# A conditional fallback and its branch hints: a constant hint on five engines against a register hint on two

## The chip, the cores and the metric

One core of one Trainium2 chip. The metric is the time of one execution in device microseconds; the profile's span of the same execution is 1.7 to 1.9 us shorter.

## The reference

Two attention blocks over the same input, mixed by a gate (batch 1, sequence 2048, width 512, 32 heads of 16):

```python
g = sigmoid((x * gate_w).sum(-1, keepdims=True))
a = full_softmax_attention(x, A_wqkv, A_wo)
b = sliding_attention(x, B_wqkv, B_wo)      # window 8, dilation 2
return g * a + (1 - g) * b
```

## The kernel before

A fast path of some 21,000 instructions computes everything, and also a flag that says whether its approximations were safe. Behind it stands an exact version of the whole computation, which runs only if the flag is set. With these inputs it is not set, so each engine loads the flag, jumps over a long body and ends. A branch hint is an instruction ahead of that branch, 49 to 56 ns long in the traces, that names the branch and a direction. A branch that has none is called a miss below: from its start to the engine's next instruction it takes longer than the 0.47 to 0.60 us with a hint.

```python
    with ExitStack() as c1:
        _Fast(c1, tc, aps, flag).build()
    cond = nc.values_load(flag[0:1, 0:1], min_val=0, max_val=1)
    with tc.If(cond > 0, label="exact"):
        tc.strict_bb_all_engine_barrier()
        with ExitStack() as c2:
            _build_exact(c2, tc, aps)
```

The head of the fast path loads x from two engines' queues, warms PE up with zeros and makes a zeroed tile for that:

```python
        nc.sync.dma_start(out=self.x_tiles[0][:, 0:2, :], in_=self.x_src[:, 0:2, :])
        nc.scalar.dma_start(out=self.x_tiles[0][:, 2:4, :], in_=self.x_src[:, 2:4, :])
        self.load_w("A", "q", 0)
        # ... cut: five more loads on SyncE, the gate vector last
        self.wz = c([P, P], BF16, name="wz")
        nc.vector.memset(self.wz[:, 0:P], 0.0)
        warm = self.wk.tile([P, 1], F32, name="warm")
        nc.vector.memset(warm[:], 0.0)
        nc.scalar.activation(out=warm[:], in_=warm[:], func=ACT.Exp)
```

In the body ScalarE runs 687 softmax activations, 628 of them behind a wait instruction of their own in this trace. The hint is placed from the loop that emits the instruction streams, at half of the work:

```python
            if p >= 1024 and not hinted:
                hinted = True
                tc.mark_branch_hint_location("exact", hint="LikelyTaken",
                                             engines=[ENG.SP, ENG.Activation, ENG.DVE, ENG.PE, ENG.Pool])
```

Of the kernel before, what the change touches and what calls it, by code (L numbers as in the profile page):

```python
# [11 lines left out]
ENG = mybir.EngineType  # L12
# [4 lines left out]
I32 = mybir.dt.int32  # L17
# [81 lines left out]
def _build_exact(ctx, tc, aps):  # L99
# [232 lines left out]
    if True:  # L332
# [76 lines left out]
        def b_softmax_ops():  # L409
# [46 lines left out]
            def fin():  # L456
# [4 lines left out]
                B["er_d"] = tc.dram_tile([P, WIN * 512 + 1024], BF16, name="er_dram")  # L461
                nc.sync.dma_start(out=B["er_d"][:], in_=er[:])
            return ([(setup, 0.8)] + [(mxw(w), 0.45) for w in range(2, WIN)] + [(sub(w), 0.4) for w in range(WIN)]
                    + [(exp_, 0.1)] + [(sumw(w), 0.7) for w in range(1, WIN)] + [(rcp(k), 0.5) for k in range(8)]
                    + [(fin, 1.2)])
# [289 lines left out]
class _Fast:  # L755
# [15 lines left out]
    def setup(self):  # L771
        nc, tc, ctx = self.nc, self.tc, self.ctx
# [68 lines left out]
        warm = self.wk.tile([P, 1], F32, name="warm")  # L841
        nc.vector.memset(warm[:], 0.0)
        nc.scalar.activation(out=warm[:], in_=warm[:], func=ACT.Exp)

        pidx = c([P, 1], I32, name="pidx")
        pi2 = c([P, 1], I32, name="pi2")
# [641 lines left out]
    def run(self):  # L1488
        nc, tc = self.nc, self.tc
# [8 lines left out]
        p = 0  # L1498
# [385 lines left out]
            return t["PE"] + 0.25  # L1884

        guard = 0
        hinted = False
        while True:
            guard += 1
            assert guard < 2000000  # L1890
# [13 lines left out]
                    moved = True  # L1904
            if p >= N and not self.steps and not aq and not any(pvq) and cur == NB:
                break
            if p >= 1024 and not hinted:
                hinted = True
                tc.mark_branch_hint_location("exact", hint="LikelyTaken",
                                             engines=[ENG.SP, ENG.Activation, ENG.DVE, ENG.PE, ENG.Pool])  # L1910
            eng = min(t, key=lambda e: t[e])
            now = t[eng]
            others = min(v for e, v in t.items() if e != eng)
# [205 lines left out]
```

## Time and profile before

| | before |
|---|---|
| time, median of 3 (later 4) runs | 703.44 us (703.24) |
| span in the profile | 701.2 us |
| first softmax activation | 9.28 us |
| ScalarE's last output issue | 696.64 us |
| busy: PE, ScalarE, VectorE | 97, 97, 94% |

Three stretches matter: the head up to the first softmax activation, the body from there to ScalarE's last output issue, and the tail from that issue to the end. Sequencer work (hints, branches, waits, loads of registers) is not counted as busy; it shows in the views by source line. There an engine's name with a q behind it is its sequencer.

### The profile page before, as it was taken

To read this page: it belongs to the slowest core of one execution; us is meant where nothing else is said; L and a number is where in the kernel's file an instruction comes from. 1 tells how busy PE (TensorE), PEld (TensorE's weight loads), DVE (VectorE), ACT (ScalarE), POOL (GpSimd) and SP (SyncE) were. 2 spreads that over 40 slices of the span, in tenths; PEclk is the share of its full clock that TensorE was granted. 3 is DMA by queue.
4 is the path that set the end of the run, shared out by engine and by line. 5 is a ranking of instruction groups with operands and counts; after the bars stand their busy time and mean duration, and the time that the engine had idled before them with its cause. 6 is when DMAs were issued, how large, how long until landed. Compare 5 with 4: busy or idle time off the path is not lost.

```text
span 701.2 us, 21355 instructions
## 1 busy us (share of the span) xinstructions
PE 681.1 (97%) x8578; PEld 218.6 (31%) x8578; DVE 658.5 (94%) x1099; ACT 677.9 (97%) x701; POOL 422.0 (60%) x358
## 2 busy tenths in 40 slices
PE   8999999999999999999999999999999999999996
PEld 4432222233332333233322232322222332222443
DVE  5999999998789999999999999999999999999975
ACT  5999999999999999999999999999999999999993
POOL 3556667677477545645557486676745765656680
PEclk9999999999999999999999999999999999999999
DMA  6001100000100100000003436355554553556641
GB/s 174 5 12 39 39 9 21 14 2 8 36 2 13 28 1 4 7 3 8 4 8 82 127 84 169 91 154 144 132 141 110 151 138 90 146 138 146 144 112 42
DMA packets 64486, 48.67 MB, mean 69 GB/s; under 512 B 22528, under 2 KB 64000, under 8 KB 64256
## 3 DMA queue, kind: packets, MB, share of 16 engines
q1 hardware_dynamic: 63680, 45.83, 25.5%
q8 instruction: 68, 1.11, 0.6%
q0 software_dynamic: 288, 1.05, 0.5%
q10 hardware_dynamic: 416, 0.39, 0.2%
q14 instruction: 34, 0.28, 0.2%
HBM read 39.85 MB, written 5.26 MB: 64 GB/s over the span
## 4 chain that ended last, share of the span: by engine, by line
PE 54%; ACT 30%; issue 7%; DVE 5%; DMA 2%; SPq 1%; POOL 1%; ACTq 0%; POOLq 0%
ACT pt L1931 29%; PE fps L1872 19%; PE fps L1645 18%; PE fps L892 13%; DVE yb L1564 2%; PE fps L1857 1%; PE fps L1243 1%; PE fps L1378 1%; DMA erb<-er_dram 1%; DMA v_dram<-vs 1%; DVE er L1298 1%; SPq L1328 1%; DVE yb L1573 1%; ACT er L1248 0%; DMA vw<-v_dram 0%
## 5 line engine op out<-in xcount | busy, mean ns | idle before, releaser
L1931 ACT ACTIVATE pt<-fps 128x1024 bf16<-128x1024 f32 (+1 forms) x687 | 672.0, 1137 | 6.3 <-PE fps L1872 3.9
L1564 DVE TENSOR_SCALAR yb<-fps 128x512 int16<-128x512 f32 x589 | 382.1, 681 | 16.0 <-PE fps L1872 11.4
L1872 PE MATMUL fps<-qm,kT 32*128 32x512 bf16 x1968 | 285.7, 383 | 11.4 <-ACT pt L1931 7.4
L1645 PE MATMUL fps<-pt,vaug 128*32 128x512 bf16 (+1 forms) x1557 | 233.8, 372 | 0.1
L1571 POOL TENSOR_TENSOR yb<-yb,pc 128x1024 int32<-128x1024 int32 (+2 forms) x98 | 181.3, 1861 | 71.1 <-DVE yb L1564 25.1
L1645 PE MATMUL fps<-yb,vaugw 128*32 128x512 f16 (+1 forms) x1238 | 173.1, 374 | 0.3
L1872 PEld LDWEIGHTS <-kT 32*128 32x128 bf16 x1968 | 80.6, 91 | 274.3 <-issue 269.7
L1573 DVE TENSOR_SCALAR yb<-yb 128x2048 int16<-128x2048 int16 (+2 forms) x206 | 136.9, 688 | 0.6
L1645 PE MATMUL fps<-yb,vaug 128*32 128x512 f16 (+1 forms) x619 | 103.4, 374 | 0.1
L1360 POOL TENSOR_TENSOR erb<-erb,vw 128x512 bf16<-128x512 bf16 x64 | 72.6, 1154 | 46.6 <-DVE yb L1573 33.7
L892 PE MATMUL fps<-xT,ww 128*32 128x512 bf16 (+2 forms) x1296 | 99.1, 380 | 0.0
L1360 POOL TENSOR_TENSOR er<-er,vw 128x512 bf16<-128x512 bf16 x64 | 72.6, 1155 | 36.5 <-DVE yb L1573 29.1
L1645 PEld LDWEIGHTS <-vaug 128*32 128x32 bf16 x2176 | 65.8, 94 | 80.1 <-issue 72.5
L1645 PEld LDWEIGHTS <-vaugw 128*32 128x32 bf16 x1238 | 44.7, 94 | 42.0 <-issue 36.3
L1229 POOL TENSOR_TENSOR prod<-bq,bk 128x512 bf16<-128x512 bf16 x32 | 34.3, 1075 | 29.6 <-DVE yb L1573 15.2
L892 PEld LDWEIGHTS <-ww 128*32 128x32 bf16 x1296 | 25.4, 95 | 31.3 <-issue 24.8
L1857 PE MATMUL fps<-qm,kz 128*32 128x512 bf16 x320 | 34.5, 382 | 0.5 <-DVE yb L1564 0.2
L927 POOL TENSOR_SCALAR vaugw<-vaug 128x128 bf16<-128x128 bf16 (+1 forms) x24 | 20.4, 850 | 21.5 <-DVE vaug L920 14.1
L1678 POOL TENSOR_TENSOR t<-t,rc 128x512 bf16<-128x512 f32 x15 | 15.9, 1057 | 28.6 <-DVE yb L1573 14.7
L1229 DVE TENSOR_TENSOR prod<-bq,bk 128x2048 bf16<-128x2048 bf16 x24 | 29.3, 1247 | 0.0
L1668 DVE STREAM_TRANSPOSE t<-fps 128x512 f32<-128x512 f32 x32 | 22.6, 707 | 2.1 <-PE fps L1645 2.1
L892 PE MATMUL fps<-woB,oB 128*32 128x512 bf16 x256 | 19.7, 382 | 0.0
(118 smaller groups left out, 307.8 us busy)
## 6 DMA issues: line engine op xcount, KB each, us to landing
vw<-v_dram SPq DMA_DIRECT2D x128, 128.0 KB, 3.0
er<-er_dram SPq DMA_DIRECT2D x128, 64.0 KB, 3.0
erb<-er_dram SPq DMA_DIRECT2D x128, 64.0 KB, 3.0
v_dram<-vs SPq DMA_DIRECT2D x16, 128.0 KB, 2.9
qm<-qs SPq DMA_DIRECT2D x112, 16.0 KB, 1.8
out_dram<-ob SPq DMA_DIRECT2D x13, 128.0 KB, 1.7
x_in<-in_A_x_dram SPq DMA_DIRECT2D x3, 512.0 KB, 6.8
ww<-in_B_wqkv_dram SPq DMA_DIRECT2D x12, 128.0 KB, 2.8
```

The costliest lines, as they stand in the source:

```text
L892: self.nc.tensor.matmul(out=out_ps[32 * c:32 * c + 32, 0:n], lhsT=lhsT_of(c), rhs=rhs, start=start, stop=stop, tile_position=(0, 32 * c))
L927: return self.nc.gpsimd.tensor_scalar(out=self.vw4[k][:, KD.index(st), h0:h1, 0:DH], in0=self.vaug4[:, st, h0:h1, 0:DH], scalar1=PW_W[k], ...
L1229: return e.tensor_tensor(out=pr[m % 2][:, a:b], in0=bq[ct][:, a:b], in1=bk[ct][:, o + a:o + b], op=ALU.mult)
L1360: return nc.gpsimd.tensor_tensor(out=st_["erb"][m % 4][:, g, :], in0=st_["erb"][m % 4][:, g, :], in1=st_["vw"][m % 2][:, g, :], op=ALU.mult)
L1564: return nc.vector.tensor_scalar(out=self.yb[bt["buf"]][:, 0, i * 512:(i + 1) * 512], in0=bank[:], scalar1=A, scalar2=1024.0 * (15.0 + PW_ ...
L1571: return nc.gpsimd.tensor_tensor(out=y[:, k, 0:n].bitcast(I32), in0=y[:, 0, 0:n].bitcast(I32), in1=self.pc[:, k:k + 1].to_broadcast([P, n ...
L1573: return nc.vector.tensor_scalar(out=y[:, k, 0:n], in0=y[:, 0, 0:n], scalar1=float(round(1024.0 * (PW_S[k] - PW_S[0]))), scalar2=None, op0 ...
L1645: nc.tensor.matmul(out=out, lhsT=v, rhs=r, start=start, stop=stop, tile_position=(0, 32 * j))
L1668: nc.vector.transpose(out=self.t1[:, par].rearrange("p a b -> p (a b)"), in_=self.flex[acc[b]])
L1857: nc.tensor.matmul(out=dst[32 * c:32 * c + 32, :], lhsT=self.kz[:, j, KZ.index(kt), 32 * c:32 * c + 32], rhs=self.qm[(4 * ct + qc) % NQM][ ...
L1872: nc.tensor.matmul(out=dst, lhsT=self.kT[ct % 2][32 * j:32 * j + 32, kt * 128:(kt + 1) * 128], rhs=self.qm[(4 * ct + qc) % NQM][par][32 * ...
L1931: nc.scalar.activation(out=self.pt[pi[0]][pi[1]][:, 0:n * 512], in_=self.aslot[si][:, 0:n, :].rearrange("p a b -> p (a b)"), func=ACT.Exp, ...
```

## The change

The intent: keep hints where a missed branch would be late at the end (SyncE and ScalarE), drop them elsewhere, and get them out of the way of the first loads. A hint with a constant value depends on nothing, and in the trace of before all five stand at 0.70 to 0.82 us; a hint with a register's value comes after the load of that register.

```diff
         nc.vector.memset(warm[:], 0.0)
         nc.scalar.activation(out=warm[:], in_=warm[:], func=ACT.Exp)
+        far = [ENG.SP, ENG.Activation]
+        zero = nc.values_load(self.wz[0:1, 0:2].bitcast(I32), engines=far, min_val=0, max_val=1)
+        tc.mark_branch_hint_location("exact", hint=zero, engines=far)
 ...
-            if p >= 1024 and not hinted:
-                hinted = True
-                tc.mark_branch_hint_location("exact", hint="LikelyTaken",
-                                             engines=[ENG.SP, ENG.Activation, ENG.DVE, ENG.PE, ENG.Pool])
```

## The prediction

> **What bounds the kernel now.** I read the page first, then the chain of waits over the first 10 us, then the groups by source line of the two lines that the change touches, and last the DMA view of the final 6 us. From the page:
>
> ```profile
> span 701.2 us, 21355 instructions
> PE 681.1 (97%) x8578; PEld 218.6 (31%) x8578; DVE 658.5 (94%) x1099; ACT 677.9 (97%) x701; POOL 422.0 (60%) x358
> PE 54%; ACT 30%; issue 7%; DVE 5%; DMA 2%; SPq 1%; POOL 1%; ACTq 0%; POOLq 0%
> ```
>
> Three engines are busy 94 to 97% of the span and pass the chain to one another. A branch hint is sequencer work, not engine work, so the body (about 17 to 690 us) can only be moved by it, not shortened. What is left is the head, where nothing is busy yet, and the tail, where everything is finished and the conditional fallback ("exact") is jumped over. The hint in the source stands deep in the program (at item 1024), and one would look for it in mid-span. The view by line finds it elsewhere (columns: count, shortest/median/longest ns, first and last start):
>
> ```profile
> L2114 POOLq BRANCH_PREFETCH_HINT  x1: 51/51/51, 0.7 to 0.7; - x1
> L2114 ACTq BRANCH_PREFETCH_HINT  x1: 50/50/50, 0.7 to 0.7; - x1
> L2114 SPq BRANCH_PREFETCH_HINT  x1: 56/56/56, 0.7 to 0.7; - x1
> L2114 DVEq BRANCH_PREFETCH_HINT  x1: 51/51/51, 0.8 to 0.8; - x1
> L2114 PEldq BRANCH_PREFETCH_HINT  x1: 50/50/50, 0.8 to 0.8; - x1
> ```
>
> All five stand at 0.7 to 0.8 us, as the first thing after the start barrier: a constant hint depends on nothing, and the scheduler has floated it to the front. That makes the odd wording of the change plain: a hint whose value is a loaded register must follow that load, and the load follows the DMA issues ahead of it. In the chain and timeline of the head (start us, length, what):
>
> ```profile
> 0.70 0.05 POOLq L2114
> ...
> 0.82 0.48 ACTq L825 DMA_DIRECT2D x_in<-in_A_x_dram  x1
> 0.85 0.46 SPq L824 DMA_DIRECT2D x_in<-in_A_x_dram  x1
> ...
> 5.17 1.16 PEld L983 LDWEIGHTS <-x_in 128*128 128x128 bf16 x16 [1.41 <-DMA x_in<-in_A_x_dram]
> ```
>
> SyncE's load of the first half of x is issued at 0.85 us and lands after 4.3 us (its line's issue-to-landing), so at 5.15; PE's first transpose starts at 5.17. That is the path of the head. The page's chain names POOL's memsets there, but PE needs of POOL only the identity, ready at 1.39, so I read it as the DMA. The tail, by the line of the branch and of the program's end:
>
> ```profile
> L750 SPq COMPARE_BRANCH  x1: 70/70/70, 696.9 to 696.9; - x1
> L750 DVEq EVENT_SEMAPHORE  x1: 21/21/21, 697.0 to 697.0; - x1
> L750 ACTq EVENT_SEMAPHORE  x1: 17/17/17, 698.3 to 698.3; - x1
> L750 SPq EVENT_SEMAPHORE  x9: 17/17/17, 697.4 to 699.5; - x9
> ...
> L2114 POOLq EVENT_SEMAPHORE  x4: 17/17/17, 700.4 to 701.1; - x4
> L2114 PEldq DRAIN  x2: 8/8/8, 696.4 to 700.7; - x2
> L2114 DVEq DRAIN  x2: 10/14/17, 697.2 to 700.7; - x2
> L2114 ACTq DRAIN  x2: 8/8/8, 698.4 to 700.7; - x2
> ```
>
> The last output is issued by ScalarE at 696.64 and lands 2.8 us later, at 699.4. SyncE waits for it, walks its semaphores to 700.4, and POOL, which gathers all five engines, goes on at 700.4 and ends at 701.2. PE has been waiting there since 696.4, VectorE since 697.2, ScalarE since 698.4, POOL since 684.7. So the slack of the branch is 4.0 us on PE, 3.2 on VectorE, 2.0 on ScalarE, about 15 on POOL; on SyncE about 1.5, from 697.4 to the landing less its earlier waits.
>
> [...]
>
> **The change part by part.**
>
> Removed: five constant hints at the front. Each takes 0.05 us plus about 0.06 to the next instruction. On SyncE the start barrier ends near 0.68, the hint starts at 0.74 and the load at 0.85: without it the load can start at 0.74, a gain of 0.11 us. On ScalarE it goes from 0.82 to 0.74, a gain of 0.08. PE waits for both halves; SyncE's lands last (5.15 against 0.82 + 4.0 = 4.82), so the head gains 0.11 at most. I take 0.08 to 0.10, as the transfer need not start sooner by all of it. POOL's identity and VectorE's zero tile also come 0.1 us sooner, off the path.
>
> Added on ScalarE: a register load from the zeroed tile, then the hint. The same kind of load of the flag took 0.702 us on ScalarE. It sits after the warm-up activation (2.63 to 2.83), and ScalarE's next work is at 6.32 with 3.49 us idle before it. Some 0.9 us in that hole costs nothing.
>
> Added on SyncE: a load (0.541 for the flag), what followed the flag load there, register operations 0.192 and an assertion 0.029, the hint 0.056, and four gaps of about 0.06: 1.06 us. In the order of the code it comes behind the tiny gate vector's load, which ends at 8.05. The next issue, branch B's first weights at 8.10, moves to about 9.1; then SyncE waits anyway, for VectorE's K at line 971, 12.2 us in the longest case. B's weights are not needed in the head. Cost 0.
>
> Tail, ScalarE and SyncE: still hinted, as before, 0.4 to 0.5 us from branch to next instruction. PE, VectorE and POOL lose theirs[...]. What that costs no unhinted branch here shows; I estimate it from fetches that are there. Between 696 and 702 us:
>
> ```profile
> q14 instruction: 3, 0.02, 1.2%
> q8 instruction: 1, 0.02, 1.0%
> ```
>
> Narrower windows put the one on q8 at 696.9 to 697.1, after PE's branch ends at 696.23, and those on q14 at 697.9 to 698.1, 698.1 to 698.9 and 698.9 to 699.1, after the branches of VectorE, SyncE and ScalarE (end 696.53, 696.98, 697.89). So a fetch that such a step sets off moves data 0.7 to 1.4 us later. The shares give 1.0 us for PE's packet and 0.4 for one of the others. A miss is then about 1.7 to 2.1 us from branch to next instruction, in place of 0.06 on PE and 0.5 on VectorE, an extra of about 2 us and 1.5 us. Against slacks of 4.0 and 3.2 that is hidden. POOL has 15. Cost 0.
>
> Sum: -0.10 (head) + 0 + 0 + 0 (tail) = -0.1 us of 703.44, which makes 703.3.
>
> **The rivals.**
>
> First, the miss takes the place of the hint on the path. If one costs 3.5 us instead of 2 (two blocks one after the other, say), VectorE reaches its drain at about 696.5 + 3.5 + 0.15 = 700.2 and is still just in time; at 4 us it is 0.3 late, and PE at 4.0 is at its limit. It would add 0.2 to 0.5: 703.6. For it: 2 us is an estimate without an unhinted branch in the trace. Against it: the gaps of fetches above.
>
> Second, the hint costs more than its 0.05 us: an armed hint could hold back an instruction block, so that streams stall at block borders. PE streams 67 blocks, and 0.1 us each would give back 6.7 us (696.7). Against it: PE's idle is assigned to data, it is busy 97%, and the page's idle for matmuls is a fraction of a microsecond in nearly every group but the 11.4 us before line 1872, released by ScalarE. I give it 3%.
>
> Third, the 0.1 us at the head is swallowed, because a landing depends on all the loads together (the DMA engines are full from about 4 us on: nines in the view) or because ScalarE's load waits behind its table load and delays the copy at 6.32. It makes 703.4 or, at worst, 703.9.
>
> Fourth, the register hint arrives with a wrong sense, or does not arm, so that SyncE misses too. SyncE then goes on at about 699 instead of 697.4, still before the landing at 699.4, with nine waits of 0.07 us behind: +0.2 to +0.5.
>
> **Range and chances.** The three runs of before lie within 0.68 us (703.04 to 703.72), more than the whole expected effect. I predict 703.3, with 702.6 to 703.9 holding 8 in 10: run-to-run scatter of 0.3 either way, the first and fourth rival above, a full gain and some luck of timing below. Two per cent is 14 us; nothing here reaches it: faster 0.01, same 0.98, slower 0.01.
>
> **What would show it.** Head: no hint before the first loads, which start at about 0.74; PE's first transpose at about 5.07; the hints on SyncE near 9 us and on ScalarE between 2 and 5 us, and none elsewhere. Body: the same groups with the same durations, the same chain. Tail: from branch to next instruction about 2 us on PE and VectorE, unchanged on ScalarE and SyncE; POOL going on about 1 us after the last landing, as now. It is wrong if PE or VectorE drains after SyncE (the miss is on the path), if the copy at 6.32 moves later (the added load is on the path), or if the body itself gets shorter.

Read in the trace of before: 68 packets of 16 KB on PE's instruction queue (hence the second rival's 67 blocks) and 34 of 8 KB on the other; 65 to 84 ns for the compare-and-branch on four engines, 410 ns on PE; 1.7 to 2.8 us for the landing of the output writes. That an unhinted branch must first fetch its target was my assumption, and the 1.7 to 2.1 us for a miss are my estimate from the packets that follow the branches in the trace of before.

## The result, and the profile after

The changed kernel took 703.50 us (703.15 to 704.02, 4 runs), the kernel before 703.24 us (702.89 to 703.72, 4 runs): ratio 1.0004, 95% interval 0.9986 to 1.0021, the same. In a second set of 5 rounds it was 703.26 against 703.01, ratio 1.0006 (0.9992 to 1.0020).

From the page of the changed kernel:

```profile
span 701.6 us, 21356 instructions
PE 681.9 (97%) x8578; PEld 219.3 (31%) x8578; DVE 658.7 (94%) x1099; ACT 678.4 (97%) x701; POOL 422.6 (60%) x358
...
q8 instruction: 69, 1.13, 0.7%
...
q14 instruction: 36, 0.29, 0.2%
```

Nothing here tells the two apart, except one more block on PE's instruction queue (69 for 68) and two more on the other (36 for 34). The hints in the view by line (columns: count, shortest/median/longest ns, first and last start), and the first loads and transposes in the timeline (start, length, what):

```profile
L2112 ACTq BRANCH_PREFETCH_HINT  x1: 49/49/49, 1.9 to 1.9; - x1
L2112 SPq BRANCH_PREFETCH_HINT  x1: 56/56/56, 8.5 to 8.5; - x1
```

```profile
0.75 0.48 ACTq L825 DMA_DIRECT2D x_in<-in_A_x_dram  x1
0.75 0.45 SPq L824 DMA_DIRECT2D x_in<-in_A_x_dram  x1
...
4.18 1.49 PEld L986 LDWEIGHTS <-x_in 128*128 128x128 bf16 x16 [0.49 <-DMA x_in<-in_A_x_dram]
```

SyncE's hint stands at 8.5 us, near the forecast; ScalarE's at 1.9, a little before the 2 to 5 us forecast, because its load started at 1.33 us, while the activation table was loading (1.25 to 2.53 us), and not behind the warm-up activation. The first loads start 0.07 and 0.10 us sooner. But PE's first transpose starts at 4.18 instead of 5.17 us, and the first softmax activation at 8.63 instead of 9.28: 0.65 us were won at the head, not 0.1. The branch and the program's end:

```profile
L750 SPq EVENT_SEMAPHORE  x9: 17/17/17, 697.7 to 700.0; - x9
...
L750 PEldq COMPARE_BRANCH  x1: 3595/3595/3595, 696.1 to 696.1; - x1
L750 DVEq COMPARE_BRANCH  x1: 72/72/72, 696.7 to 696.7; - x1
...
L750 ACTq EVENT_SEMAPHORE  x1: 17/17/17, 698.2 to 698.2; - x1
...
L750 DVEq EVENT_SEMAPHORE  x1: 21/21/21, 699.9 to 699.9; - x1
...
L2112 POOLq EVENT_SEMAPHORE  x4: 17/17/17, 700.9 to 701.5; - x4
```

The compare-and-branch itself took 45 to 84 ns on the other four engines in the profiles read by line; on PE its record is 405 to 415 ns long with a hint and 3.4 to 3.9 us without one. The unhinted branch holds PE for 3.6 us and VectorE for 3.1 (696.75 to 699.90). SyncE still ends last, at 700.8, so both are hidden; VectorE's drain at 700.01 leaves 0.84 us. The last output lands 2.87 us after its issue (before: 2.76), and from that landing to the end both kernels take 1.83 us.

So the head won 0.65 us, the tail lost 0.1 to a slower landing, and yet the span grew by 0.4: the body must have lost 0.96 us, from 687.35 to 688.31. Both kernels issue the same engine instructions in the same order there. To find the place I set the 687 softmax activations of the two traces side by side. Their difference is constant to 0.01 us for tens of microseconds and then steps (time in the kernel before; difference, changed minus before, median over 16 us):

| at, us | 25 | 40 | 55 | 95 | 120 | 160 | 185 | 350 | 400 | 540 | 565 | 630 |
|---|---|---|---|---|---|---|---|---|---|---|---|---|
| difference, us | -0.65 | -0.65 | -0.44 | -0.44 | -0.23 | -0.21 | +0.07 | +0.07 | -0.13 | -0.11 | +0.10 | +0.30 |

Losses of 0.2 to 0.3 near 45, 107, 170, 550 and 615 us, a win of 0.2 between 350 and 400. These are times at which an 8 KB instruction block was fetched, a packet of 8,192 bytes on an instruction queue (45.9, 107.3, 170, 234.5, 298.5, 359.9, 422.6, 488.4, 551, 616, 681 us in the kernel before). Counted in the trace, ScalarE's 63rd recorded instruction and every 128th after it start 0.4 to 1.3 us before these fetches, and in the other profiles too about 1 us before; such a place, every 128 instructions, is called a block border below. (That the border lies behind the 63rd, and not one place off, is read from the delays themselves.) The timeline around the first border was then read by line. A window of the changed kernel, and one of the kernel before:

```profile
L1929 ACT ACTIVATE pt<-fps x2: 1024/1058/1092, 43.1 to 44.3; 128x1024 bf16<-128x1024 f32 x2
L1929 ACTq EVENT_SEMAPHORE  x1: 17/17/17, 44.0 to 44.0; - x1
```

```profile
L1931 ACT ACTIVATE pt<-fps x2: 1087/1089/1091, 43.8 to 44.7; 128x1024 bf16<-128x1024 f32 x2
L1931 ACTq EVENT_SEMAPHORE  x1: 17/17/17, 44.6 to 44.6; - x1
```

Two activations follow one another after 0.9 us before, and after 1.2 us in the changed kernel, where the second one comes 0.4 us behind the wait that released it instead of 0.1. ScalarE's stream had one hint ahead of these, and has a load and a hint now: every later instruction stands one place further on. That is the theory which the experiments had to test: **the block border now falls between a wait and the activation that it holds back, where the crossing is exposed; before it fell behind an activation, where the activation's own 0.9 us hid it.** The rivals: chance; SyncE's three added instructions; the missing hints on PE, VectorE and POOL.

### The profile page after: what moved, and what is told of

It is laid out like the page before. It is cut to its first block, busy times and chain, and to the rows that moved or that the text cites. A ratio compares the mean times of both kernels' runs of the same rounds, so it can differ in the third digit from the quotient of the medians. Undisturbed runs are those within 1.5% of the kernel's fastest.

```text
span 701.6 us, 21356 instructions
## 1 busy us (share of the span) xinstructions
PE 681.9 (97%) x8578; PEld 219.3 (31%) x8578; DVE 658.7 (94%) x1099; ACT 678.4 (97%) x701; POOL 422.6 (60%) x358
## 4 chain that ended last, share of the span: by engine, by line
PE 51%; ACT 31%; issue 7%; DVE 7%; DMA 2%; SPq 1%; POOL 0%; ACTq 0%
ACT pt L1929 30%; PE fps L1875 18%; PE fps L1648 17%; PE fps L895 12%; DVE yb L1567 3%; PE fps L1860 1%; DMA erb<-er_dram 1%; PE fps L1381 1%; PE fps L1246 1%; DVE yb L1576 1%; SPq L1331 1%; DVE er L1301 1%; PE fps L980 1%; ACT er L1251 0%; DMA vw<-v_dram 0%
```

## The experiments

Twelve runs (two of them repeats); all gave correct results. "Body" runs from the first softmax activation in the expectations that put it at 686 to 689 us. In those that put it at 672 to 674, and in the table here, it runs from the thirteenth (the text there says twelfth, as it counted from zero), because one kernel lost 0.4 us behind the second activation that has nothing to do with borders. Tail: ScalarE's last output issue to the end. "Half of x": when the later of the two halves was complete. Shift: places by which ScalarE's stream is moved against before.

| kernel | shift | time, us (before beside it) | ratio (95%) | half of x | 13th softmax | body | tail |
|---|---|---|---|---|---|---|---|
| before | 0 | 703.24 | | 5.13 | 24.25 | 672.39 | 4.58 |
| before, repeated | 0 | 702.58 (703.01) | 0.9996 (0.9982-1.0010) | 4.96 | 24.39 | 672.39 | 4.97 |
| changed | +1 | 703.50 (703.24) | 1.0004 (0.9986-1.0021) | 4.56 | 23.59 | 673.35 | 4.70 |
| changed, repeated | +1 | 703.26 (703.01) | 1.0006 (0.9992-1.0020) | 4.51 | 23.26 | 673.28 | 4.92 |
| no hint | -1 | 704.14 (703.01) | 1.0020 (1.0006-1.0033) | 4.40 | 23.15 | 672.86 | 5.68 |
| three hints put back | +1 | 703.71 (703.01) | 1.0010 (0.9997-1.0024) | 4.56 | 24.16 | 673.25 | 4.91 |
| before + 1 filler | +1 | 703.83 (702.99) | 1.0014 (0.9999-1.0030) | 4.86 | 23.73 | 673.37 | 4.78 |
| changed + 7 fillers | +8 | 702.91 (702.99) | 0.9999 (0.9985-1.0012) | 4.41 | 23.64 | 672.57 | 4.84 |
| ScalarE's hint in front | 0 | 702.99 (702.99) | 1.0000 (0.9987-1.0014) | 4.36 | 23.52 | 672.34 | 5.07 |
| SyncE's hint in front | +3 | 704.24, one run | | 4.84 | 24.34 | 673.40 | 4.69 |
| changed + 1 filler | +2 | 702.79 (702.90) | 0.9996 (0.9983-1.0010) | 4.43 | 23.72 | 672.70 | 4.78 |
| two hints in front alone | 0 | 703.04 (702.90) | 1.0002 (0.9988-1.0016) | 4.84 | 23.70 | 672.59 | 4.69 |
| the same, ScalarE's load later | 0 | 702.67, one run | | 4.51 | 23.26 | 672.65 | 4.97 |
| changed + 1 filler, drains | +2 | 703.47, one run | | 5.01 | 24.13 | 672.59 | 4.96 |

The times alone separate hardly anything; the traces separate it to some hundredths of a microsecond. Starts, bodies and tails are sums over instruction start times in the traces.

**The kernel before again.** No edit.

> The kernel before, once more, for the scatter. If executions of one kernel are as regular as the two traces suggest (the start times of ScalarE's activations in the two kernels differ by a constant to 0.01 us for tens of microseconds, then step), then this profile against the first profile of before shows no steps in the body beyond 0.05 us, and the time is within 0.3 us of its pair. If the steps are chance, this pair of profiles shows steps of 0.1 to 0.3 us too. PE's first transpose: at 5.17 us again if the landing of x is regular; anywhere between 4.6 and 5.2 if it is chance.

The start of the body moved by +0.14 us, and then the difference to the first profile of before stayed at 0.13 to 0.14 for all 660 us: no step. Body 672.39 in both. So chance did not touch the body between these two profiles, and a delay at the head was carried to the last instruction in full. Chance sits in the head (the landing of x and the speed of the first transposes) and in the last landing, which here took 3.15 us instead of 2.76. In the chain of waits of this profile the load of x, not POOL, leads to the first transposes, as the prediction had read it:

```profile
0.85 4.11 DMA x_in<-in_A_x_dram
4.96 0.05 issue
5.01 1.62 PE fps L983 x16
```

**The changed kernel again.** No edit.

> The changed kernel once more, for the scatter and for the ratio. Theory A (the head gains, the body loses by chance): the steps in the body against the first profile of this kernel are as large as between the two kernels. Theory B (the change has moved ScalarE's instructions by one place, and stalls at the borders of its fetch blocks have moved with them): no steps against its own first profile, and the same steps of +0.2 to +0.28 near 45, 107 and 170 us against before. Time 703.2 to 703.9 in both.

Against its own first profile the difference was -0.34 us at 25 us and -0.40 at 660, without a step above 0.1; against before it had the same steps at the same places. Body 673.28. Chance as the cause of the lost 0.9 us is out.

**No hint.**

```diff
-        far = [ENG.SP, ENG.Activation]
-        zero = nc.values_load(self.wz[0:1, 0:2].bitcast(I32), engines=far, min_val=0, max_val=1)
-        tc.mark_branch_hint_location("exact", hint=zero, engines=far)
```

> No hint at all and no register load. Every engine misses: 3.1 to 3.6 us from branch to next instruction, as PE (3.6) and VectorE (3.1) show in the changed kernel. SyncE's branch ends near 697.0, so it goes on near 700.1 instead of 697.4; its landing is at 699.4, and seven waits of 0.08 us now stand behind the miss: the tail is longer by about 1.2 us. ScalarE's branch ends near 697.8, so it drains near 701.0, about 0.15 before SyncE then. Theory: 1.0 to 1.4 us slower in the tail than the changed kernel, 704.6 or so. Rival (a miss costs nothing as it lies under the last landing on all engines): within 0.2 us of the changed kernel.

The only kernel that is clearly slower than before, by 0.2%. By line of the branch:

```profile
L750 SPq EVENT_SEMAPHORE  x9: 17/17/17, 699.4 to 700.0; - x9
...
L750 SPq COMPARE_BRANCH  x1: 45/45/45, 696.3 to 696.3; - x1
L750 ACTq COMPARE_BRANCH  x1: 54/54/54, 697.2 to 697.2; - x1
...
L750 ACTq EVENT_SEMAPHORE  x1: 17/17/17, 699.8 to 699.8; - x1
```

SyncE needs 3.1 us to its next instruction, ScalarE 2.6. SyncE comes back at 699.42, after the last landing at 699.21, and has all its waits still before it: from the landing to the end it takes 2.48 us instead of 1.83. My 1.2 us was too much, as the miss outlasts the landing by 0.21 us and not by 0.7; with seven waits of 0.066 us behind it that makes the 0.65. ScalarE drains at 699.88, in time. So of the two hints that the change keeps, SyncE's is shown to be worth 0.65 us; that ScalarE's is needed is not shown. The body (shift -1) is 0.47 longer than before, at other borders in part, as one expects if the stream moves the other way.

**Three hints put back**: the changed kernel plus the constant hints of VectorE, PE and POOL.

```diff
         tc.mark_branch_hint_location("exact", hint=zero, engines=far)
+        tc.mark_branch_hint_location("exact", hint="LikelyTaken", engines=[ENG.DVE, ENG.PE, ENG.Pool])
```

> The changed kernel with the constant hints of VectorE, PE and POOL put back at the front: what the removal alone does. The misses of VectorE and PE go (0.4 to 0.5 us from branch to next instruction on VectorE, 0.06 on PE). If they are hidden as I predicted: the tail from the last output issue to the end is within 0.05 us of the changed kernel's. If the fetches of the missed targets slow the last output's writes (its landing took 2.89 us against 2.77 before): the tail is 0.1 us shorter. The head: SyncE and ScalarE issue at 0.75 as in the changed kernel, so PE's first transpose at the same time as there.

The misses went (PE's branch 405 ns, VectorE 0.60 us to its next instruction), and the last landing to the end stayed at 1.83 us: a removal that is hidden. Nor did the landing become shorter (3.08 us), so that suspicion, that the misses slow the last writes, has no support: 2.76 and 3.15 us without misses (before), 2.87 and 3.10 with them (the changed kernel). Body 673.25, steps as in the changed kernel: the missing hints on these three engines are not the cause. The head missed my expectation: x was there at 4.56, as in the changed kernel, but PE's 16 transposes took until 6.38 instead of 5.84. With the changed kernel's head, this kernel's first softmax activation came at 9.19 us, hardly before that of before (9.28).

**Before plus one filler**: one small activation more on ScalarE, no other change.

```diff
         nc.scalar.activation(out=warm[:], in_=warm[:], func=ACT.Exp)
+        for _ in range(1):
+            nc.scalar.activation(out=warm[:], in_=warm[:], func=ACT.Copy)
```

> The kernel before with one more small activation on ScalarE (a 128x1 copy behind the warm-up), and nothing else. Every later ScalarE instruction moves one place against its 128-instruction fetch blocks, as in the changed kernel; SyncE, VectorE, PE and POOL keep their streams and their hints. I count body from the first softmax activation to ScalarE's last output issue: 687.36 and 687.35 us in two profiles of before, 688.31, 688.25 and 688.22 in the changed kernel twice and in the mixed one. Theory (block borders on ScalarE): 688.2 to 688.3, with the same steps near 45, 107, 170, 381, 420, 550 and 615 us as the changed kernel shows. Rival (SyncE's load, hint and assertion, or SyncE's stream, cause the steps): 687.35 and no steps. Head as in before.

Body 673.37 from the thirteenth activation (688.34 from the first), 0.98 more than before, with the steps of the changed kernel: SyncE's stream, all five hints and everything else are those of before. One 128x1 activation at the start, in an idle hole, costs 1 us 40 to 600 us later. So the shift of ScalarE's stream alone does it. (The head was not as in before: the first softmax activation came at 8.76 us.) The first border of this kernel, by line, in the same form as above:

```profile
L1933 ACT ACTIVATE pt<-fps x2: 1023/1058/1092, 43.3 to 44.5; 128x1024 bf16<-128x1024 f32 x2
L1933 ACTq EVENT_SEMAPHORE  x1: 17/17/17, 44.1 to 44.1; - x1
```

**The changed kernel plus one filler** (the same edit on it):

> The changed kernel with one small activation more on ScalarE, so that its stream has shift +2 against before, an even one. Body from the twelfth softmax activation to ScalarE's last output issue: 672.39 in both profiles of before and 672.34 in the kernel with shift 0; 673.35, 673.28, 673.25 and 673.37 with shift +1; 673.40 with +3; 672.86 with -1; 672.57 with +8. Borders between a wait and its activation: the same 4 of 11 as before. Theory: 672.3 to 672.5, no step of +0.2 at 45, 107 or 170 us, although this kernel has everything that the changed one has. Rival (what the changed kernel adds costs the 0.9 us in some other way): 673.3. Time 0.9 us below the changed kernel by theory, 702.4 to 702.8.

The window around the same time in this kernel, which has everything that the changed one has:

```profile
L1931 ACT ACTIVATE pt<-fps x2: 1087/1088/1090, 43.3 to 44.2; 128x1024 bf16<-128x1024 f32 x2
L1931 ACTq EVENT_SEMAPHORE  x1: 17/17/17, 44.1 to 44.1; - x1
```

0.9 us from activation to activation, and no step at 45, 107 or 170 us (difference to before -0.52 at 25 us, -0.54 at 185, -0.53 at 290). The body is 672.70, 0.6 us shorter than the changed kernel's, so the filler mends most of it. It misses the 672.3 to 672.5 by 0.2, through smaller steps from 296 us on. Three of them, of 0.14 to 0.16 us near 296, 487 and 680, stand at this kernel's own borders, which fall before other activations than in before, and are in part won back; those near 424, 438 and 447 stand at no border of ScalarE's, and their cause is open.

**The changed kernel plus seven fillers**: the same edit with range(7).

> The changed kernel with seven more small activations on ScalarE in its idle hole at the start. From the order of ScalarE's records in the profile of before I counted how many of its 11 block borders fall between a semaphore wait and the activation that it holds back, for each shift of the stream against before: 4 of 11 for shift 0, 7 for +1 (the changed kernel), 6 for -1 (no hint), 9 for +9, and 2 for +8, which is this kernel. The bodies so far give (688.25 - 687.36) / 3 = 0.30 us for each such border more. Theory: 687.36 - 2 x 0.30 = 686.8 us of body (686.7 to 687.0). Rival (the body depends on something else than the shift, for example on the two instructions before the activations): 688.25 as in the changed kernel. Time 1.4 us below the changed kernel if the head does not lose; seven activations of 0.2 us end near 4.5 us, before ScalarE's copy at 5.3 to 5.7.

A partial miss. Body 672.57, 0.75 below the changed kernel, but not 0.6 below before: the two borders (near 298 and 681 us) that the shift freed gave nothing, and a step of +0.24 appeared at 484, at a border of this kernel's own between a wait and its activation. A border between the two thus doesn't always cost. The start times say where it does. In all fourteen profiles, an activation with such a border before it starts 0.34 to 0.65 us after its wait; where another kernel has no border before the same activation, it starts 0.05 to 0.83 us after it. Where it would have come late anyway, there is nothing to lose: near 234 us it takes 0.61 in the changed kernel and in before, near 681 us 0.65 in both. Near 44, 106, 169, 550 and 615 us it takes 0.34 to 0.39 in the changed kernel and 0.06 to 0.15 in before. Summed over its borders, the excess is 1.43 us in the changed kernel and 0.66 in before, and the difference, 0.77, is most of the lost 0.96. One thing stays open: near 298 us the border delays the activation in before by 0.30 (0.35 for 0.05), and yet the kernels without it win nothing there. So counting borders gave the sign, and the delay at each one most of the size.

**ScalarE's hint in front, SyncE's behind its loads:**

```diff
-        far = [ENG.SP, ENG.Activation]
+        far = [ENG.SP]
         zero = nc.values_load(self.wz[0:1, 0:2].bitcast(I32), engines=far, min_val=0, max_val=1)
         tc.mark_branch_hint_location("exact", hint=zero, engines=far)
+        tc.mark_branch_hint_location("exact", hint="LikelyTaken", engines=[ENG.Activation])
```

> SyncE's hint behind the loads by a register as in the changed kernel, ScalarE's as a constant at the front, as in before. ScalarE's stream has shift 0: theory says a body of 687.35 us (against 688.25 in the changed kernel). Head: SyncE issues its half of x at 0.75 and ScalarE at 0.82, so SyncE is first. If the order of the two issues decides when the halves land (in before ScalarE issues 0.03 us ahead, SyncE's packets begin 1.9 to 2.1 us after its issue, and the later half lands at 4.5 to 4.9; in the four kernels in which SyncE is not behind, 4.2 to 4.3), the later half lands at 4.2 to 4.4. If any hint ahead of a load costs the 0.5 us, 4.5 to 4.9. Sum 702.3 or so.

The body is 672.34 from the thirteenth activation, as said; from the first it is 687.72, because behind the second activation 0.41 us of the early start were lost (the first starts 1.14 us earlier than before, the third 0.73). The head answers the second question. SyncE issues at 0.75, ScalarE, behind its hint, at 0.83, and all of x is there at 4.36: the hint ahead of ScalarE's load cost nothing here. Time 702.99, 0.7 above the 702.3 expected: the 0.41 us are one part, and the last landing took 3.24 us, longer than before's 2.76.

**The mirror image**: far is ScalarE alone, and SyncE's hint is the constant one.

> The mirror image: SyncE's hint constant at the front, ScalarE's by a register behind its load. ScalarE issues at 0.75, SyncE at 0.85. Order theory: the later half of x lands at 4.5 to 4.9 as in before, although ScalarE's own load is early. Rival (each hint costs only its own 0.1 us): 4.2 to 4.4. ScalarE's stream has shift +3 (the load brings two register operations along when SyncE does not load), 7 borders of 11: body 688.2 to 688.3.

ScalarE issues at 0.75, SyncE at 0.86, and x is complete at 4.84, as in before, though ScalarE's half is there at 4.24. Second place on SyncE goes with the late landing here, not the hint's own 0.1 us. But so far every kernel with SyncE in second place also had a hint ahead of SyncE's load; the last two runs part them. The body, shift +3, is 673.40.

**Two hints in front alone**: the hints of PE, VectorE and POOL removed, those of SyncE and ScalarE constant; no load.

```diff
-        zero = nc.values_load(self.wz[0:1, 0:2].bitcast(I32), engines=far, min_val=0, max_val=1)
-        tc.mark_branch_hint_location("exact", hint=zero, engines=far)
+        tc.mark_branch_hint_location("exact", hint="LikelyTaken", engines=[ENG.SP, ENG.Activation])
```

> One part alone: the hints of PE, VectorE and POOL removed, those of SyncE and ScalarE left constant at the front, no register load. ScalarE's stream has shift 0. Body 672.3 to 672.4. Head: ScalarE issues at 0.82, SyncE at 0.85, so the later half of x lands as in before (all 16 parts at 4.9 to 5.1, SyncE's; 3.7 to 4.2 where SyncE issued first). Tail: PE and VectorE miss for 2.9 to 3.9 us from the branch, hidden: 1.83 us from the last landing to the end, as in every kernel with a hint on SyncE. Time equal to before's within 0.3 us.

x is complete at 4.84, misses of 3.6 us on PE and 2.9 on VectorE are hidden (1.83 us from landing to end), and no step stands at 45, 107, 170, 550 or 615 us. The body has 0.2 too much, in small steps near 423, 449 and 625 us, like the filler kernel above; open. Time 703.04 against 702.90: equal.

**The same with ScalarE's load later**: SyncE keeps its hint ahead of its load, but is first.

```diff
-        nc.scalar.dma_start(out=self.x_tiles[0][:, 2:4, :], in_=self.x_src[:, 2:4, :])
 ...
         nc.scalar.activation(out=warm[:], in_=warm[:], func=ACT.Exp)
+        nc.scalar.dma_start(out=self.x_tiles[0][:, 2:4, :], in_=self.x_src[:, 2:4, :])
```

> The kernel with two constant hints in front alone, and ScalarE's half of x issued behind its warm-up activation instead of ahead of it (at some 1.0 to 1.4 us instead of 0.82). SyncE still has its hint ahead of its load and issues at 0.85, but is now first. So far, being second and having a hint in front went together on SyncE in all five slow profiles. If being second is what costs: SyncE's half is complete at 3.8 to 4.3 us (3.75 to 4.18 where SyncE was first or level; its packets start on the mean at 2.6 to 2.9). If the hint in front of SyncE's load costs it: 4.8 to 5.1, packets at 3.6 to 3.8, as in the five slow ones.

In the timeline (start, length, what):

```profile
0.85 0.46 SPq L824 DMA_DIRECT2D x_in<-in_A_x_dram  x1
...
1.00 0.43 ACTq L843 DMA_DIRECT2D x_in<-in_A_x_dram  x1
...
3.81 0.31 PEld L984 LDWEIGHTS <-x_in 128*128 128x128 bf16 x2
```

SyncE's half, issued at 0.85 behind a hint, lands after 2.9 us, at 3.72, and PE starts on it at 3.81. All of x is there at 4.51, although ScalarE issued 0.18 us later than before.

**The filler kernel with two drains ahead of SyncE's first load**: no hint in front, but SyncE second.

```diff
+        nc.sync.drain()
+        nc.sync.drain()
         nc.sync.dma_start(out=self.x_tiles[0][:, 0:2, :], in_=self.x_src[:, 0:2, :])
```

> The changed kernel with one filler, and two drains (empty waits) on SyncE ahead of its first load, which should put that off by some 0.1 us, without a hint in front. SyncE is then second to ScalarE at 0.75. If being second costs: SyncE's half is complete at 4.8 to 5.1 us. If the hint costs: 3.9 to 4.3. If the drains are dropped and SyncE still issues at 0.75, the run says nothing.

The timeline of this kernel:

```profile
0.74 0.48 ACTq L827 DMA_DIRECT2D x_in<-in_A_x_dram  x1
...
0.85 0.45 SPq L826 DMA_DIRECT2D x_in<-in_A_x_dram  x1
...
5.05 1.16 PEld L990 LDWEIGHTS <-x_in 128*128 128x128 bf16 x16 [1.37 <-DMA x_in<-in_A_x_dram]
```

Issued at the same 0.85, without a hint, SyncE's half lands after 4.2 us. So it is the order of the two issues and not the hint, as far as one profile of each of these two kernels can show it. Over the fourteen profiles: where ScalarE issues first, if only by 0.03 us, x is complete at 4.84 to 5.13 (six profiles, 4.94 on the mean); where SyncE is first or level, at 4.36 to 4.56 (eight, 4.47 on the mean). The trace's transfer records have SyncE's first 256 packets of 1 KB, its half of x, at 3.64 to 3.72 us on the mean in the former and at 2.57 to 2.75 in the latter. Why the queue that comes second waits so long, no run here shows. Both kernels have even shift and bodies of 672.6.

**Is there a better version?** By the traces, the change with an even shift, or ScalarE's hint in front, has the early head and the short body. The kernels of shift +1 had ratios to before of 1.0004, 1.0006, 1.0010 and 1.0014, those of even shift 0.9996 to 1.0002; but no interval of these excludes 1. None beats before beyond the scatter of 0.3 to 0.8 us that head and last landing bring along.

## Why the prediction was right or wrong

The time (703.3, measured 703.50) and the verdict were right. Two steps of the sum were wrong and in large part cancelled (in the first profiles -0.65 us at the head against +0.96 in the body), so it was right in part by luck. The sign, 0.1 us faster, cannot be told from the scatter.

- **Head, -0.10: mis-sized.** Issue times came out as said (0.75 for 0.74). The first softmax activation came 0.65 us earlier, and 0.99 in the repeat. The failed step is "so the head gains 0.11 at most": it took the two landings as independent and moved each by its own issue. The order of the two issues changed as well, from ScalarE first to level, and that brought x 0.4 to 0.6 us sooner. The rest is the speed of PE's first transposes: 16 of them took 1.3 and 1.6 us in the chains of before, 1.25 in the changed kernel, and 14 took 0.95 in its repeat. In the traces they start every 0.11 us up to the moment at which the first record of a full granted clock begins, and every 0.06 us after it. That record begins at 5.75 and 6.22 us in the two profiles of before, at 5.22 and 3.89 in those of the changed kernel, and at 6.58 in the kernel with three hints put back. It thus moves by 1.3 us between two profiles of one kernel, and nothing shows that the change moves it: this part of the gain is chance as far as is known. The heads overlap accordingly: the first softmax activation comes at 8.74 to 9.42 us in the six profiles with SyncE second and at 8.14 to 9.19 in the other eight.
- **Loads and hints on ScalarE and SyncE, 0: right as to their time, wrong as to their place.** ScalarE's load and hint lay at 1.3 to 1.9 us under the activation table's load (and not behind the warm-up activation), SyncE's before a wait of 6.8 us. But the two instructions in place of one moved ScalarE's stream by one, and that cost 0.9 to 1.0 us in the body.
- **Body: "it can only be moved by it, not shortened".** The failed step. The second rival came near, since it looked at block borders; it looked for the cause in an armed hint and on PE, and argued against itself with PE's idle. The page's idle would not have shown it on ScalarE either: 6.8 us in place of 6.3 before line 1929. What shows it is two traces laid on one another.
- **Tail, misses hidden: right; their size was wrong.** Estimated at 1.7 to 2.1 us from branch to next instruction, measured 2.6 to 3.9 in the kernels with a miss (PE 3.5 to 3.9, VectorE 2.9 to 3.4, SyncE 3.1, ScalarE 2.6). The packet came as estimated: on PE's instruction queue one begins 1.0 us after the branch's start and ends after 1.9 to 2.4 us in all ten profiles with a miss there (with the hint, in before, one also begins 1.1 us after the start and ends after 2.1). What the estimate had no term for is the time from the packet's end to the next instruction, 1.5 to 1.6 us. What the packet carries and what the engine waits for after it, the traces do not show. The first rival's 3.5 us came nearer, though the trace has one block in that time and not two. Of the slack of 3.2 us on VectorE 0.84 was left.
- **Fourth rival, the register hint doesn't arm: out.** SyncE and ScalarE needed 0.52 and 0.48 us in both kernels.
- **Third rival, the gain is swallowed: out as such.** Head delays were carried through the whole body. In one kernel 0.41 us of a very early head were lost behind the second activation.

## What to carry to other kernels

In this kernel, with PE and ScalarE busy 97% of the span, one instruction more ahead of ScalarE's long unrolled stream moved all its later instructions against its fetch blocks of 128. That cost 0.9 to 1.0 us in 700, more than the change itself; the streams of PE, VectorE and POOL, which lost their hint, lost nothing by it (body 672.34 in the kernel with ScalarE's hint in front, at shift 0, against 672.39 before). So compare such variants at equal shift, with a filler if need be. Two profiles of one kernel tell first how much is chance; the running difference of the start times of one engine's instructions then shows where a change gains or loses, at a hundredth of the scatter of the total. And look where a hint really lands in the trace: a constant one was at 0.70 to 0.82 us, not where the source has it.
